# First transform stages of a long convolution: float32 operands in half-row pairs instead of rounded high and low parts

## The chip, the core and the metric

One core of one Trainium2 chip. The metric is the device time of one execution in microseconds, median of several runs; the kernel before was run three times. Lower is better. TensorE appears as PE, VectorE as DVE, ScalarE as ACT, GpSimd as POOL, SyncE as SP. The profile of the kernel before comes from one further execution.

## What is computed

The reference adds three parts over 2048 tokens of 512 channels. Only the first is touched by the change; the second fills most of TensorE's time.

```python
xn = _layernorm(A_q)
# A: gated long convolution
k_shift = sum over t of k_pad[:, t:t+S] * shift_k[:, 3 - t]      # 4 taps
kv = k_shift * v
y  = irfft(rfft(pad(kv)) * rfft(pad(ssm_k)))[:S] + kv * ssm_D    # 4096-point transforms by channel
a  = xn * y
# B: top-2 of 8 experts, D = 512, F = 1792
b  = sum over e of gate_e * (silu(xn @ w1[e]) @ w2[e])
out = A_q + a + b
```

## The kernel before, in words

**Experts.** `build` (L1073) runs a lead-in (loading, logits, routing) and then eight experts one after another (`expert`, L913). The tokens of each expert are gathered, transposed (`turn`, L840: tiles `xg`, `ptm` or `ptx`, `xh`, `xl`) and multiplied with weight slices (`weights`, L882: a slice `wraw` comes by SP's queue, ACT makes its rounded part `wh`, DVE the rest `wl`; for slices 1 to 5 of the first expert POOL makes `wl`). Every product is three float32r products (`mm6`, L902): high by high, high by low, low by high. ACT then makes `h` and `ht` from the product tile `ps`, of which there are two; so the product of a feature block f (48 matmuls for f=0 and f=1 together in the first expert) has to be read by ACT before that of f+2 can start.

**The convolution in the background.** The transforms are done as matrices: a first stage over 64 points (the filter by `conv_k`, L646; the gated tokens by `conv_v`, L682), a middle stage by 32 groups (`group_unit`, "g"), a last stage of 16 units (`last_unit`, "l"). After the last of these, `merge` adds what the experts left in `acc_d` to the output. From the twentieth feature block on, `fill` (L1138) hands out pieces of these units between the experts' matmuls, by the costs in `WORK`: the sum of all costs is spread evenly, and what is left when the last expert begins is issued at once. Six of the eight units of `conv_k` are issued earlier, in the lead-in and the routing, two in the background; all eight of `conv_v` are in the background. The scheduler then sets the order on each engine.

**The first stage of the filter.** A unit of `conv_k` transposes eight blocks of 128x128 (`ptk`), splits them into a rounded part `kh` (ACT) and a rest `kl` (DVE, or POOL in the three units before the routing, where ACT also makes an unrounded copy `kr`), and multiplies: four product tiles of 512 columns with three float32r matmuls each, 12 in all, with weights `ek` that hold zeros in one half of their rows.

**The first stage of the tokens.** A unit of `conv_v` makes the tile `kva` by eight DVE operations, splits it by halves of its partitions into two tiles `vp` (two ACT casts, two DVE subtractions L733), and multiplies (`stage1`, `edge1`): four product tiles with two float32r matmuls each, 8 in all. ACT evicts each product to `ev`, and SP stores it to `zk_d` or `zv_d`. `ptk`, the products and other small products share four PSUM tiles (pool `pc`); `kh`, `kl`, `kva`, `vp`, `ev` and the routing tables (`slots`) share seven SBUF tiles (tag `b4`).

**The lead-in.** DVE computes the routing in one long chain; TensorE makes its small products (`pw`, `ptab`); ACT computes one Exp (`gt`, L456); POOL gathers six blocks `xg`, makes two `wl` (L895) and normalizes 12 blocks of `x` (L317). Then DVE and ACT scale `xg` (L875, L873), TensorE transposes it and the first expert's matmuls (L910) begin.

Of the kernel before, what the change touches and what calls it, by code (L numbers as in the profile page):

```python
# [11 lines left out]
F32 = mybir.dt.float32  # L12
F32R = mybir.dt.float32r
# [5 lines left out]
P = 128  # L19
S = 2048  # L20
D = 512
DC = D // P
# [21 lines left out]
WORK = {"k": 1.7, "v": 12.6, "g": 5.0, "l": 2.8}  # L44
# [19 lines left out]
def fft_constants():  # L64
# [12 lines left out]
    fh, fl = _split(fwd.reshape(N1, P))  # L77
# [4 lines left out]
    zf, zi = np.zeros_like(fl), np.zeros_like(il)  # L82
    first = np.zeros((N1, 2, 2, 2, P), np.float32)
    for h in range(2):
        first[:, h, 0, h], first[:, h, 1, h] = fh, fl
    edge = np.concatenate([first.reshape(P, 4 * P), np.concatenate([fh, fh]), np.concatenate([fl, zf]),
                           np.concatenate([zf, fl]), il, ih, il, zi, ih, zi], axis=1)
# [57 lines left out]
class Builder:  # L145
# [47 lines left out]
    def load_x(self, ep, sp, cp):  # L193
# [139 lines left out]
    def routing(self, bp, sp, cp):  # L333
# [113 lines left out]
        for dc, c8 in ((1, 1), (2, 0), (2, 1)):  # L447
            for _ in self.conv_k(cp, dc, c8, True):
                pass
# [153 lines left out]
    def split_halves(self, pair, src):  # L603

        nc = self.nc
        halves = [slice(h * H, (h + 1) * H) for h in range(2)]
        for w, t in zip(halves, pair):
            nc.scalar.activation(t[w], src[w], AF.Copy)
        for w, o, t in zip(halves, halves[::-1], pair):
            nc.vector.tensor_sub(t[o], src[w], t[w])  # L610

    def edge1(self, out, h, pair):

        self.nc.tensor.matmul(out, self.ev[:, 0, :], pair[h], start=True, stop=False)
        self.nc.tensor.matmul(out, self.ev[:, 1 + h, :], pair[h], start=False, stop=True)
# [5 lines left out]
    def stage1(self, cp, pair, zd):  # L621
        nc = self.nc
        _, m, w = pair[0].shape
        for h in range(2):
            ev = cp.tile([P, m, w], F32, tag="b4", name="ev")
            for i in range(2):
                r = slice(i * m // 2, (i + 1) * m // 2)
                ps = self.pc.tile([P, m // 2, w], F32, tag="c", name="ps1")
                self.edge1(ps, h, [t[:, r, :] for t in pair])
                nc.scalar.activation(ev[:, r, :], ps, AF.Copy)  # L630
            nc.sync.dma_start(zd[h], ev)

    def load_k(self, cp, dc):

        nc, io = self.nc, self.io
        if dc == 0:
            self.dv = self.cp.tile([P, DC], F32, name="dv")
            nc.sync.dma_start(self.dv, io["A_ssm_D"].rearrange("(c p) -> p c", p=P))
        t = cp.tile([P, S], F32, tag="k8", name="ks", bufs=2)
        if dc == DC - 1:  # L640
            self.after(nc.gpsimd.memset(t[:1, :1], 0.0), self.gather, "the first expert's tokens come first")
        nc.sync.dma_start(t, io["A_ssm_k"][dc * P:(dc + 1) * P, :])
        nc.gpsimd.tensor_add(t[:, 0:1], t[:, 0:1], self.dv[:, dc:dc + 1])
        return t.rearrange("p (n i) -> p i n", i=NI)

    def conv_k(self, cp, dc, c8, routed):  # L646

        nc = self.nc
        if c8 == 0:
            self.ks = self.load_k(cp, dc)  # L650
        ks = self.ks
        parts = []
# [531 lines left out]
```

## Time and profile before

| | us |
|---|---|
| median of 3 runs | 884.62 (881.83 to 886.33) |
| the profiled execution | 887.87 |
| its span, first to last instruction | 885.9 |
| PE busy | 846.9 (96%) |
| DVE busy | 618.8 (70%) |
| ACT busy | 522.1 (59%) |
| POOL busy | 241.3 (27%) |

The span is from the first to the last instruction on the core; 2 us of the execution lie outside it. Busy times are summed over the span. A matmul's record is longer than the distance to the next one, since matmuls overlap at their ends: what a matmul costs TensorE is read from the distance of starts.

### The profile page before, as it was taken

The numbers are of one execution on the slowest core, as the hardware profiler recorded it, in microseconds if no ns is written. First come the engines' busy times: TensorE is split into PE (matmuls) and PEld (weight loads), VectorE is DVE, ScalarE is ACT, GpSimd is POOL, SyncE is SP. The second block draws the span as 40 slices with busy tenths as digits, with TensorE's granted clock in tenths as the row PEclk, the third lists the DMA queues.
The fourth block names the chain that finished last, engine by engine and source line by source line (L and its number), as shares of the span: only waits on it lengthen the run. The fifth ranks groups of instructions, "written<-read, shape, count | busy, mean of one in ns | idle before, by whom it ended". The sixth has DMA issues, their size and how long they took to land. (4 is left out here: it accounts for less than half of the span.)

```text
span 885.9 us, 13938 instructions
## 1 busy us (share of the span) xinstructions
PE 846.9 (96%) x5072; PEld 753.6 (85%) x5072; DVE 618.8 (70%) x867; ACT 522.1 (59%) x808; POOL 241.3 (27%) x209
## 2 busy tenths in 40 slices
PE   9849899999999999999999999999999999997996
PEld 7538899999999999899999888888888787885885
DVE  6977583499879988277775787577865866996421
ACT  4637342356644565477865877658865776775420
POOL 1383205055320723005020052123001401553422
PEclk9969999999999999999999999999999999998999
DMA  8569745988989675756676567558556738998972
GB/s 324 165 199 357 281 162 156 246 190 235 234 199 254 203 223 175 251 159 207 189 222 205 176 201 243 175 168 289 190 165 188 221 109 259 306 303 240 312 192 70
DMA packets 146641, 191.37 MB, mean 216 GB/s; under 512 B 12689, under 2 KB 106251, under 8 KB 145100
## 3 DMA queue, kind: packets, MB, share of 16 engines
q1 hardware_dynamic: 130204, 147.23, 54.3%
q0 software_dynamic: 16368, 43.24, 17.0%
q8 instruction: 41, 0.67, 0.3%
q14 instruction: 28, 0.23, 0.1%
HBM read 144.27 MB, written 50.63 MB: 220 GB/s over the span
## 5 line engine op out<-in xcount | busy, mean ns | idle before, releaser
L892 ACT ACTIVATE wh<-wraw 128x1024 fp32r<-128x1024 f32 (+1 forms) x116 | 119.4, 1030 | 140.9 <-PE ps L910 85.1
L895 DVE TENSOR_TENSOR wl<-wraw,wh 128x1024 fp32r<-128x1024 f32 (+1 forms) x111 | 131.7, 1187 | 97.8 <-ACT wh L892 88.8
L910 PE MATMUL ps<-xh,wh 128*128 128x512 f32 (+4 forms) x672 | 183.9, 327 | 6.3 <-ACT ht L937 5.9
L910 PE MATMUL ps<-xh,wl 128*128 128x512 f32 (+4 forms) x672 | 183.2, 326 | 0.0
L910 PE MATMUL ps<-xl,wh 128*128 128x512 f32 (+4 forms) x672 | 183.2, 326 | 0.0
L910 PE MATMUL ps<-h,wh 128*128 128x288 f32 (+3 forms) x896 | 155.2, 291 | 0.0
L910 PEld LDWEIGHTS ps<-h,wh 128*128 128x128 f32 x896 | 129.9, 188 | 1.7
L910 PEld LDWEIGHTS ps<-xh,wh 128*128 128x128 f32 x672 | 114.3, 190 | 17.7 <-ACT ht L937 7.5
L910 PEld LDWEIGHTS ps<-xh,wl 128*128 128x128 f32 x672 | 114.1, 190 | 9.6
L910 PEld LDWEIGHTS ps<-xl,wh 128*128 128x128 f32 x672 | 114.3, 190 | 9.2
L938 DVE TENSOR_TENSOR h<-ht,h 128x512 fp32r<-128x512 f32 (+4 forms) x112 | 81.7, 731 | 28.4 <-ACT ht L937 27.6
L936 ACT ACTIVATE h<-ps 128x512 fp32r<-128x512 f32 (+4 forms) x112 | 67.9, 606 | 53.5 <-PE ps L910 49.8
L910 PE MATMUL ps<-h,wl 128*128 128x288 f32 (+3 forms) x448 | 94.6, 290 | 0.0
L984 PE MATMUL py<-wh,h 128*128 128x512 f32 x224 | 87.6, 391 | 0.0
L983 PE MATMUL py<-wl,h 128*128 128x512 f32 x224 | 87.6, 391 | 0.0
L982 PE MATMUL py<-wh,h 128*128 128x512 f32 x224 | 87.1, 392 | 0.2 <-ACT ht L937 0.2
L964 POOL DMA_INDIRECT acc_d<-acc,ids x36 | 48.5, 1346 | 97.2 <-DVE acc L962 89.9
L835 POOL DMA_INDIRECT xg<-xn_d,gix x34 | 48.7, 1433 | 93.9 <-PE ptx L854 47.6
L910 PEld LDWEIGHTS ps<-h,wl 128*128 128x128 f32 x448 | 71.6, 189 | 0.5
L949 POOL DMA_INDIRECT acc<-acc_d,gix x36 | 44.2, 1227 | 96.6 <-PE ptx L854 59.6
L937 ACT ACTIVATE ht<-ps 128x512 f32<-128x512 f32 (+4 forms) x112 | 68.3, 609 | 0.0
L743 POOL DMA_DIRECT2D mid<-in_c_mid_dram x16 | 9.3, 580 | 163.5 <-PE pz L601 157.7
(256 smaller groups left out, 1409.5 us busy)
## 6 DMA issues: line engine op xcount, KB each, us to landing
wraw<-in_B_w_dram SPq DMA_DIRECT2D x84, 512.0 KB, 4.6
wraw<-in_B_w_dram SPq DMA_DIRECT2D x32, 448.0 KB, 3.8
zk_d<-ev SPq DMA_DIRECT2D x16, 512.0 KB, 7.0
zv_d<-ev SPq DMA_DIRECT2D x16, 512.0 KB, 8.7
mid<-in_c_mid_dram POOLq DMA_DIRECT2D x16, 512.0 KB, 4.6
z<-zk_d SPq DMA_DIRECT2D x32, 256.0 KB, 2.8
z<-zv_d SPq DMA_DIRECT2D x32, 256.0 KB, 3.5
zi_d<-zo SPq DMA_DIRECT2D x32, 256.0 KB, 3.3
```

The lines of the kernel that those rows point to most:

```text
L835: self.gather = nc.gpsimd.indirect_dma_start(out=t[:sb], out_offset=None, in_=self.xn_d[:, :] if r else self.io["A_q"].rearrange("o s d -> ...
L892: w = nc.scalar.activation(hi, raw, AF.Copy)
L895: t = (lo_eng or nc.vector).tensor_sub(lo, raw, hi)
L910: nc.tensor.matmul(ps[:, u, :n], w, x[:, u, :], start=first and w is wh and k == 0, stop=last and w is wl)
L936: nc.scalar.activation(h, ps[:, :nu, :n], AF.Silu)
L937: acts.append(nc.scalar.activation(t, ps[:, :nu, :n], AF.Silu))
L938: self.hid = nc.vector.tensor_sub(l, t, h)
L949: nc.gpsimd.indirect_dma_start(out=acc[:sb], out_offset=None, in_=sum_d[:, :], in_offset=bass.IndirectOffsetOnAxis(ap=self.gix[:sb, c0 + b ...
L964: st = nc.gpsimd.indirect_dma_start(out=sum_d[:, :], out_offset=bass.IndirectOffsetOnAxis(ap=self.ids[:sb, c0 + b:c0 + b + 1], axis=0), in ...
L982: nc.tensor.matmul(o, a, wh[:, f, :], start=ff == 0, stop=False)
L983: nc.tensor.matmul(o, a, wl[:, f, :], start=False, stop=False)
L984: nc.tensor.matmul(o, l, wh[:, f, :], start=False, stop=ff == FC - 1)
```

## The change

Both first stages now multiply float32 words. `kh`, `kl`, `kr`, `vp` and the split operations are gone: a unit of `conv_k` evicts its transposed block once, unrounded (`kt`), a unit of `conv_v` uses `kva` itself. A unit of `conv_k` now takes channels of two blocks of 128 together, the upper half of the partitions belonging to one and the lower to the other, and the two halves are multiplied by two matmuls that use 64 rows each (`ev[h, :]`, `src[h, r, :]`) and write two product tiles. Four such float32 matmuls of 512 columns make a unit. The filter is loaded two blocks at a time (one tile of 2 MB for two loads; the second pair waits for the gathers). Of the eight `conv_k` units, three come in the lead-in, three with the routing, two in the background, as before. The taps are loaded and turned one unit ahead. The weights `ek` are gone, `ev` is one tile of 64 KB and comes by SP's queue instead of POOL's. `ht` and `yt` share one tag of four tiles, and the costs for `fill` are new.

```diff
-WORK = {"k": 1.7, "v": 12.6, "g": 5.0, "l": 2.8}
+WORK = {"t": 1.2, "k": 0.6, "v": 10.2, "g": 5.0, "l": 2.8}
...
-        self.ek = cp.tile([P, 2, 2, P], F32R, name="ek", bufs=1)
-        self.ev = cp.tile([P, 3, P], F32R, name="ev", bufs=1)
-        edge = io["c_edge"]
-        nc.gpsimd.dma_start(self.ek, edge[:, :4 * P].rearrange("p (a c m) -> p a c m", a=2, c=2))
-        nc.gpsimd.dma_start(self.ev, edge[:, 4 * P:7 * P].rearrange("p (a m) -> p a m", a=3))
+        self.ev = cp.tile([P, P], F32, name="ev", bufs=1)
+        nc.sync.dma_start(self.ev, io["c_edge"][:, :P])
...
+    def pairs(self, cp, src, zd):
+        nc = self.nc
+        m, w = src.shape[1:]
+        halves = [slice(h * H, (h + 1) * H) for h in range(2)]
+        evs = [cp.tile([P, m, w], F32, tag="b4", name="ev") for _ in range(2)]
+        for i in range(2):
+            r = slice(i * m // 2, (i + 1) * m // 2)
+            ps = [self.pc.tile([P, m // 2, w], F32, tag="c", name="ps1") for _ in range(2)]
+            for t, h in zip(ps, halves):
+                nc.tensor.matmul(t, self.ev[h, :], src[h, r, :], start=True, stop=True)
+            for t, ev in zip(ps, evs):
+                nc.scalar.activation(ev[:, r, :], t, AF.Copy)
+        for ev, z in zip(evs, zd):
+            nc.sync.dma_start(z, ev)
...
+        t = cp.tile([P, 2, S], F32, tag="k8", name="ks", bufs=2)
+        for c in range(2):
+            dc = 2 * pair + c
+            if pair:
+                self.after(nc.gpsimd.memset(t[:1, c, :1], 0.0), self.gather, "the first expert's tokens come first")
+            nc.sync.dma_start(t[:, c, :], io["A_ssm_k"][dc * P:(dc + 1) * P, :])
+            nc.gpsimd.tensor_add(t[:, c, 0:1], t[:, c, 0:1], self.dv[:, dc:dc + 1])
...
+        kt = cp.tile([P, 8, P], F32, tag="b4", name="kt")
         for i in range(2):
             pt = self.pc.tile([P, 4, P], F32, tag="c", name="ptk")
             for u in range(4):
...
+            nc.scalar.activation(kt[:, 4 * i:4 * i + 4, :], pt, AF.Copy)
...
-        pair = [cp.tile([P, 4, DH], F32R, tag="b4", name="vp") for _ in range(2)]
-        halves = [slice(h * H, (h + 1) * H) for h in range(2)]
-        for w, t in zip(halves, pair):
-            nc.scalar.activation(t[w], a[w], AF.Copy)
-        for w, o, t in zip(halves, halves[::-1], pair):
-            nc.vector.tensor_sub(t[o], a[w], t[w])
-            yield 1.2
         yield
-        self.stage1(cp, pair, [self.zv_d[:, NI * h + 4 * c4:NI * h + 4 * c4 + 4, ds] for h in range(2)])
+        self.pairs(cp, a, [self.zv_d[:, NI * h + 4 * c4:NI * h + 4 * c4 + 4, ds] for h in range(2)])
...
-                t = hp.tile([P, nu, n], F32, tag="ht", name="ht", bufs=2)
+                t = hp.tile([P, nu, n], F32, tag="ht", name="ht", bufs=DC)
...
-            t = hp.tile([P, nu, n], F32, tag="yt", name="yt", bufs=DC)
+            t = hp.tile([P, nu, n], F32, tag="ht", name="yt", bufs=DC)
```

The order on the engines moves at three places. In the lead-in, POOL and ACT before (POOL first; `kl`, `kr`, `kh` belong to `conv_k`, `gt` is the Exp, `wh` a weight slice):

```order
L643 TENSOR_TENSOR ks<-ks,dv 128x1 x2
L669 TENSOR_TENSOR kl<-kr,kh 128x512 x5
L643 TENSOR_TENSOR ks<-ks,dv 128x1
L669 TENSOR_TENSOR kl<-kr,kh 128x512
L835 DMA xg<-in_A_q_dram,gix 96x512 x6
L662 ACTIVATE kh<-ptk 128x512 x2
L892 ACTIVATE wh<-wraw 128x1024 x2
L456 ACT_TABLE_LOAD
L456 ACTIVATE gt<-gt 128x16
L892 ACTIVATE wh<-wraw 128x1024
```

and now:

```order
L628 TENSOR_TENSOR ks<-ks,dv 128x1 x2
L809 DMA xg<-in_A_q_dram,gix 96x512 x6
L642 ACTIVATE kt<-ptk 128x512 x2
L866 ACTIVATE wh<-wraw 128x1024
L608 ACTIVATE ev<-ps_690 128x512
L608 ACTIVATE ev<-ps_691 128x512
L449 ACT_TABLE_LOAD
L449 ACTIVATE gt<-gt 128x16
```

POOL has no subtraction of `conv_k` ahead of its gathers any more, and the Exp stands behind one weight slice where it stood behind two.

On PE, from the transposes of the first expert's tokens (`ptm`) to its matmuls, before:

```order
L600 MATMUL ps_805<-kl,ek 128x512
L601 MATMUL ps_805<-kh,ek 128x512
L854 MATMUL ptm<-ident,xg 128x96 x6
L659 MATMUL ptk<-ident,ks 128x128 x8
L854 MATMUL ptm<-ident,xg 128x96 x6
L599 MATMUL ps_830<-kh,ek 128x512
L599 MATMUL ps_835<-kh,ek 128x512
L910 MATMUL ps<-xh,wh 128x288 x2
```

and now, inside the first expert (feature blocks f=0 and f=1 end where the first `ps_726` stands, f=2 begins behind `ps_762`):

```order
L641 MATMUL ptk<-ident,ks 128x128 x8
L884 MATMUL ps<-xl,wh 128x288
L884 MATMUL ps<-xh,wl 128x288 x2
L884 MATMUL ps<-xh,wh 128x288 x2
L884 MATMUL ps<-xl,wh 128x288 x2
L884 MATMUL ps<-xh,wl 128x288 x2
L606 MATMUL ps_726<-kt,ev 128x512
L606 MATMUL ps_727<-kt,ev 128x512
L606 MATMUL ps_732<-kt,ev 128x512
L606 MATMUL ps_733<-kt,ev 128x512
L641 MATMUL ptk<-ident,ks 128x128 x8
L606 MATMUL ps_755<-kt,ev 128x512
```

Two whole `conv_k` units have moved from before the first expert's matmuls to behind f=1, and between `ptm` and L884 nothing stands any more.

On POOL at the last expert (`xnb` is the product of a last-stage unit, `mt` and `out_dram<-mt` belong to `merge`), before:

```order
L813 TENSOR_TENSOR xnb<-xnb,yb 128x512 x10
L964 DMA acc_d<-acc,ids 2048x512 x4
L813 TENSOR_TENSOR xnb<-xnb,yb 128x512
L824 DMA mt<-acc_d 128x1024
L813 TENSOR_TENSOR xnb<-xnb,yb 128x512
L825 DMA out_dram<-mt 128x1024
L824 DMA mt<-acc_d 128x1024
L813 TENSOR_TENSOR xnb<-xnb,yb 128x512
```

and now:

```order
L787 TENSOR_TENSOR xnb<-xnb,yb 128x512 x16
L938 DMA acc_d<-acc,ids 2048x512 x4
L798 DMA mt<-acc_d 128x1024 x3
L799 DMA out_dram<-mt 128x1024 x3
L798 DMA mt<-acc_d 128x1024 x3
```

All sixteen products of the last stage now stand ahead of the seventh expert's stores and of `merge`; six of them stood among the transfers of `merge`.

## Rows read from the trace of the kernel before

**Rows 1.** Busy time by stretch: the stretch in us, its length, then for PE, PEld (weight load), DVE, ACT and POOL busy us and instructions, the granted clock as a share of 2.4 GHz, DMA share and GB/s.
```profile
180.00:360.00 180.00, 179.45 (x1385) 176.48 (x1385) 152.93 (x164) 99.32 (x154) 66.64 (x45) 1.00 0.82 214
390.00:800.00 410.00, 406.67 (x2131) 347.37 (x2130) 301.88 (x377) 293.65 (x446) 93.78 (x79) 1.00 0.67 213
800.00:820.00 20.00, 14.47 (x50) 10.36 (x50) 11.81 (x15) 9.88 (x16) 7.73 (x10) 0.85 0.80 233
```

**Rows 2.** The waits of PE, longest first: who waited for whom, us in total, times, the longest.
```profile
PE ptm L854 <- DVE xg L875: 10.2, 1, 10.2
PE ps L910 <- ACT ht L937: 5.9, 3, 4.5
```

**Rows 3.** The timeline of PE at full clock: start us, us, engine, line, operation, shapes and count. First a `conv_v` unit's float32r matmuls, then two float32 matmuls of the routing (each is one matmul in the program and two records in the trace), then a unit's transposes.
```profile
189.05 0.40 PE L614 MATMUL ps<-vp,ev 128*128 128x512 f32 x1
189.28 0.39 PE L615 MATMUL ps<-vp,ev 128*128 128x512 f32 x1
189.51 0.42 PE L910 MATMUL ps<-xh,wh 128*128 128x276 f32 x2
...
35.36 0.39 PE L380 MATMUL pw<-sel,rt 128*128 128x128 f32 x2
35.58 0.39 PE L381 MATMUL pw<-rt,cs 128*128 128x128 f32 x2
...
72.01 1.09 PE L659 MATMUL ptk<-ident,ks 128*128 128x128 f32 x8
```

**Rows 4.** Groups of PE instructions by line and shape: count, then busy us and mean ns of one, then idle time before.
```profile
L854 PE MATMUL ptx<-ident,xg 128*128 128x128 f32 x64 | 8.8, 272 | 0.0
L854 PE MATMUL ptx<-ident,xg 88*128 88x88 f32 x24 | 2.6, 239 | 0.0
```

**Rows 5.** The timeline of DVE in the lead-in; in brackets idle time before the row and who ended it.
```profile
28.46 0.29 DVE L362 TENSOR_TENSOR eq<-lgt,m 128x128 f32<-128x128 f32 x1
30.41 1.31 DVE L362 TENSOR_TENSOR eq<-L,m 128x128 f32<-128x128 f32 x1
31.64 1.25 DVE L454 TENSOR_TENSOR gt<-m,m 128x16 f32<-128x16 f32 x1
37.91 1.16 DVE L295 TENSOR_SCALAR rs<-mv 128x16 f32<-128x16 f32 x1
51.81 0.17 DVE L457 TENSOR_SCALAR gt<-gt 128x16 f32<-128x16 f32 x1 [4.25 <-ACT gt L456]
53.17 5.46 DVE L462 TENSOR_TENSOR gl<-gf,gh 128x32 f32<-128x32 f32 x1
62.50 0.16 DVE L442 COPY tb<-ptab 96x24 f32<-96x24 f32 x1
65.04 1.88 DVE L875 TENSOR_SCALAR xg<-xg,sc,sc 96x512 f32<-96x512 f32 x3
```

**Rows 6.** The timeline of POOL in the lead-in.
```profile
30.30 2.57 POOL L669 TENSOR_TENSOR kl<-kr,kh 128x512 fp32r<-128x512 f32 x2 [3.71 <-ACT kr L668]
37.75 1.28 POOL L669 TENSOR_TENSOR kl<-kr,kh 128x512 fp32r<-128x512 f32 x1
53.76 4.66 POOL L895 TENSOR_TENSOR wl<-wraw,wh 128x1024 fp32r<-128x1024 f32 x2
58.39 12.45 POOL L317 TENSOR_SCALAR x<-x,rstd,nmr 128x512 f32<-128x512 f32 x12
```

**Rows 7.** The timeline of ACT at the Exp and behind the first transposes.
```profile
45.61 1.06 ACT L892 ACTIVATE wh<-wraw 128x1024 fp32r<-128x1024 f32 x1 [2.81 <-DMA wraw<-in_B_w_dram]
49.20 1.06 ACT L892 ACTIVATE wh<-wraw 128x1024 fp32r<-128x1024 f32 x1 [2.52 <-DMA wraw<-in_B_w_dram]
74.25 2.94 ACT L314 ACTIVATE x<-x,nmr,rstd 128x512 f32<-128x512 f32 x4
```

**Rows 8.** The timeline of PE from the transposes of the tokens on: the k matmuls between them, the first matmuls of the first expert, and f=2, which begins at 82.58.
```profile
65.76 2.18 PE L854 MATMUL ptm<-ident,xg 96*128 96x96 f32 x12 [10.16 <-DVE xg L875]
67.65 1.20 PE L599 MATMUL ps<-kh,ek 128*128 128x512 f32 x2
...
71.51 0.66 PE L854 MATMUL ptm<-ident,xg 96*128 96x96 f32 x6
...
73.96 0.42 PE L910 MATMUL ps<-xh,wh 128*128 128x288 f32 x2
...
82.58 0.42 PE L910 MATMUL ps<-xh,wh 128*128 128x288 f32 x2
```

**Rows 9.** DMA issues: operation, count, KB each, median us from issue to landing.
```profile
ks<-in_A_ssm_k_dram SPq DMA_DIRECT2D x4, 1024.0 KB, 14.0
```

**Rows 10.** The timeline of POOL, ACT and PE at the last expert.
```profile
810.54 0.97 POOL L825 DMA_DIRECT2D out_dram<-mt  x1 [6.57 <-DMA xnb<-xn_d]
811.74 1.64 POOL L813 TENSOR_TENSOR xnb<-xnb,yb 128x512 f32<-128x512 f32 x1
813.41 1.21 ACT L810 ACTIVATE yb<-psb 64x512 f32<-64x512 f32 x2 [5.18 <-POOL xnb L813]
815.77 0.80 PE L910 MATMUL ps<-xh,wh 128*128 128x512 f32 x1 [4.47 <-ACT ht L937]
816.80 0.63 PE L910 MATMUL ps<-xh,wl 128*128 128x512 f32 x1
820.64 0.43 PE L910 MATMUL ps<-xh,wl 128*128 128x512 f32 x1
```

More of the change, by code (lines that the diff above doesn't have):

```diff
@@ L81, in fft_constants @@
     ih, il = _split(inv.reshape(P, N1))
[L82 to L87, printed above, removed]
+    zi = np.zeros_like(il)
+    f = fwd.reshape(N1, P).astype(np.float32)
+    edge = np.concatenate([np.concatenate([f, f]), il, ih, il, zi, ih, zi], axis=1)
     n2 = np.arange(N2)
@@ L446, in routing @@
         self.prep(0)
-        for dc, c8 in ((1, 1), (2, 0), (2, 1)):
-            for _ in self.conv_k(cp, dc, c8, True):
+        for pair, q8 in ((0, 3), (1, 0), (1, 1)):
+            for _ in self.conv_k(cp, pair, q8):
                 pass
@@ L617, in tokens @@
     def tokens(self, ap):
         return ap.rearrange("(n h j) d -> h n j d", h=2, j=NI)
[L621 to L631, printed above, removed]
@@ L633, in load_k @@
-    def load_k(self, cp, dc):
+    def load_k(self, cp, pair):
         nc, io = self.nc, self.io
-        if dc == 0:
+        if pair == 0:
             self.dv = self.cp.tile([P, DC], F32, name="dv")
             nc.sync.dma_start(self.dv, io["A_ssm_D"].rearrange("(c p) -> p c", p=P))
[L639 to L644, printed above, removed]
@@ L658, in conv_k @@
             for u in range(4):
-                nc.tensor.transpose(pt[:, u, :], ks[:, 8 * c8 + 4 * i + u, :], self.ident)
-            if routed:
-                hi, lo = (t[:, r, :] for t in big)
-                nc.scalar.activation(hi, pt, AF.Copy)
-                self.after(nc.vector.tensor_sub(lo, pt, hi), self.indexed, "the routing comes first")
-            else:
-                hi, lo, raw = (self.xp.tile([P, 4, P], d, tag="xg", name=n, bufs=10)
-                               for d, n in ((F32R, "kh"), (F32R, "kl"), (F32, "kr")))
-                nc.scalar.activation(hi, pt, AF.Copy)
-                nc.scalar.activation(raw, pt, AF.Copy)
-                nc.gpsimd.tensor_sub(lo, raw, hi)
@@ new lines, in conv_k, with load_taps @@
+            nc.scalar.activation(kt[:, 4 * i:4 * i + 4, :], pt, AF.Copy)
+        yield 0.3
+        yield
+        self.pairs(cp, kt, [self.zk_d[:, 8 * q8:8 * q8 + 8, dc * P:(dc + 1) * P] for dc in (2 * pair, 2 * pair + 1)])
+        yield 0.3
+    def load_taps(self, cp, dh):
+        ds = slice(dh * DH, (dh + 1) * DH)
+        self.sr = cp.tile([P, DH, 4], F32, tag="b4", name="shr")
+        self.nc.sync.dma_start(self.sr,
+                               self.io["A_shift_k"][ds].rearrange("(o d) t -> o d t", o=1).to_broadcast([P, DH, 4]))
@@ L707, in conv_v @@
         yield
-        if sr is not None:
-            self.sb = cp.tile([P, 4, DH], F32, tag="sb", name="sb", bufs=1)
-            nc.vector.tensor_copy(self.sb, sr.rearrange("p d t -> p t d"))
+        if dh == 1 and c4 == 0:
+            self.turn_taps(cp)
             yield 1.2
@@ L1109, in build @@
             slots = self.slots(cp)
-            units = [("k", lambda c8=c8: self.conv_k(cp, 3, c8, True)) for c8 in range(2)]
+            units = [("t", lambda: self.first_taps(cp))]
+            units += [("k", lambda q8=q8: self.conv_k(cp, 1, q8)) for q8 in (2, 3)]
             units += [("v", lambda dh=dh, c4=c4: self.conv_v(cp, dh, c4)) for dh in range(2) for c4 in range(4)]
```

52 lines of the change are left out of this document (19 added, 33 removed).

## The prediction

> **What bounds the kernel now.** I read the busy time by stretch first. Between 180 and 360 us PE is busy 179.45 of 180 us, between 390 and 800 us 406.67 of 410, at full clock [rows 1]: there the number of matmuls and their distance set the time, 1385 in 179.45 us or 0.13 us for one of the usual shape. DVE has 152.93 of the first 180 us: what it loses there (two subtractions per token unit) is hidden behind PE, and ACT, with 99.32, likewise; I cost those splits at nothing. The waits of PE come second: the longest is 10.2 us for the first expert's scaled tokens, the next 5.9 us for ACT, of which 4.5 are one wait [rows 2]. So the time has three handles: the matmul work after the first expert starts, the moment at which it starts, and that one wait near the end.
>
> **Matmul work.** Starts of the token unit's float32r matmuls lie 0.23 us apart [rows 3]. A token unit (8) costs 1.84 us, a filter unit (12) 2.76. Float32: one matmul of the program is two records, and two of them with 128 columns lie 0.22 us apart, so a record takes 0.11 [rows 3]. [...] A record of 512 columns then takes 0.44 us, a float32 matmul 0.88, and a unit of four 3.52 us if everything runs one behind the other. [...]
>
> The two matmuls of a pair use different halves of the array's rows and write different product tiles, and no wait stands between them. No row of this trace shows whether such matmuls overlap. If order on PE is kept, the second record of one can run beside the first record of the next: eight records take five slots of 0.44, 2.2 us a unit. Between 2.2 and 3.52 I take 2.2, since a matmul waits only for the one ahead to stream, not for its end (0.39 long, 0.23 apart [rows 3]), and in another half of the array nothing streams that it must wait for.
>
> [...]
>
> With 2.2 the eight token units cost 8 x 0.36 = **2.9 us more**, the two late filter units 2 x 0.56 = **1.1 us less**. Serially it is 8 x 1.68 = 13.4 more and 2 x 0.76 = 1.5 more. Against the change stands the passage from full-height to half-height matmuls and back: no row has one. Between nothing and the overlap of two neighbours lost twice (0.39 - 0.23 = 0.16 us [rows 3]) for 12 groups, that is 0 to 3.8 us; passages between matmuls and transposes show no gap at all, so I take **1.0**.
>
> [...]
>
> **The start of the first expert.** Look at DVE: the same comparison takes 0.29 us at 28.46 and 1.31 at 30.41, and two operations on 16 columns take 1.25 and 1.16 [rows 5]. Each falls into a subtraction `kl` of POOL [rows 6]; all of these are gone from POOL. I count 1.0 + 1.0 + 0.9 = 2.9 us off the chain. Next, DVE waits 4.25 us for the Exp [rows 5], which stood behind two weight casts, at 45.61 and 49.20 [rows 7], and now stands behind one: about 3.6 us earlier. Then one operation of 32 columns takes 5.46 us [rows 5] while POOL makes two `wl` [rows 6]. POOL does these behind the gathers, so they end 2.9 us earlier too, at about 55.5, but DVE by then has the rows behind the Exp done; before, it had them ahead of it, and came to the scale factors only at 62.50. Last, the three scalings of `xg`, 65.04 to 66.92 in one piece before, are now spread among some 17 small routing rows and four of 0.4 us (the scheduler's order on DVE), so that the last ends at about 62: 5 us earlier, not more. Behind it, before, 7.0 us passed until 73.96, of which 3.9 were filter matmuls between the transposes (67.65 to 71.51) [rows 8]. Those are gone from there; about 12 small DVE rows come in (1.6). So the first expert starts at 62 + 7.0 - 3.9 + 1.6 = **66.7 instead of 73.96**. Ends: only the 2.9, or 11 if DVE meets no wait for POOL.
>
> That gain isn't kept. Two filter units now stand between f=1 and f=2, and f=2 is the first point where both kernels have done the same. Before: 82.58 [rows 8]. Now 66.7, plus 48 matmuls of 0.13 (6.3), plus twice the transposes (8 in 1.09 us, 0.94 without the last one's tail [rows 3]) and a unit (2.2), 6.3 together: 79.3. To this come waits. ACT has the `x` blocks (2.94 us, rows 7), a table load and four evictions ahead of the second unit's, in one queue with the `h` of f=0 that f=2 waits for. And the filter's second pair is loaded late: SP issues it behind the read of the overflow count, about 58, and such a load took 14.0 us [rows 9], so it lands at 72 to 73 where PE wants it at 73. POOL's correction of it waits for 12.45 us of normalizing [rows 6], to about 68: hidden. I take 2.2 us (bounds 0 and 6): f=2 at 81.5, **1.1 us less** than before. With serial matmuls it is 2 x 1.32 more, of which the queue of ACT takes up a good half of the waits: about 84, 1.8 more. The stalls behind f=2, on routing tables, I leave as they are.
>
> **Near the end.** The 4.5 us wait is at 815.77: PE waits for `ht`, ACT for the tile that POOL's `xnb` frees (5.18 us), and POOL, in order, sits 6.57 us in front of a transfer of `merge` for a DMA [rows 10]. In the new order all sixteen `xnb` stand ahead of `merge`, because the last units fit before the last expert. [...] Eleven matmuls at 0.2 are 2.2. Together **6.7 less** (bounds 0 and 7). What is late next is `merge`, which starts behind all `xnb`; it has the last expert's 70 us to finish.
>
> The taps a unit ahead, `ev` by SP and four tiles for `ht` touch waits for ACT of which 1.4 us is left beside the long one [rows 2]; I cost them at nothing.
>
> **Sum**, overlapped: 2.9 - 1.1 + 1.0 - 1.1 - 6.7 = -5.0 us. The profiled execution took 887.87, 3.25 above the median of 884.62; I apply the difference to the median: **879.6**. From no change, 0.5% (4.4 us) is about what a measurement of this kernel tells.
>
> **Rivals.**
> *Serial records* (slower side). The second half-row matmul waits for the first: 13.4 + 1.5 + 1.8 + 1.0 - 6.7 = +11.0, **895.6**. For it: the records of one float32 matmul run one behind the other, and none beside another [rows 3]. Against: halves and tiles are disjoint. It decides by the cost of one float32 matmul in a saturated stretch: the sum is zero where it is some 0.68 us (the 40 late ones then take 27 us, 7 more than the 20.2 of before), 0.55 is my forecast, 0.88 the rival.
> *The end wait stays.* The last units again meet `merge`, or pile up one expert earlier, where they wait for the same two tiles: 879.6 + 6.7 = **886.3**. For it: the order is a schedule, and a unit that is late by some us meets the transfers again. Against: `xnb` stand in front of every transfer of `merge`.
> *The start is kept.* DVE and ACT run ahead enough that f=2 comes 7 us earlier as the first expert does, 6 less than summed: **873.6**; or records cost less than 0.44, which leads the same way (at 0.23 the ten late units alone would give 14 us less). For it: five us of DVE's chain are waits only. Against: ACT's queue, in which the `h` of f=0 stands last.
>
> **Numbers.** Forecast 0.47, own range 874 to 885; serial 0.25; end wait 0.15; start kept or cheap records 0.13. Faster by over 0.5% (below 880.2): somewhat over half of the forecast and all of the last, 0.40. Slower (above 889.0): most of the serial case and a little of the others, 0.25. Within: 0.35. The range goes from 870 (half of the best case left out) to 897 (a third of the serial case left out).
>
> **What would show it.** Starts of `ps<-kva,ev` records: the next pair's in the same half 0.9 us on and the partner's beside the second record means overlap; 0.44 between all means serial. `kl` gone and no DVE operation over 1 us at 30 to 38; the first L884 at 66 to 67; f=2 at 80 to 83; no wait over 2 us for `ht` near 810. I'd be wrong in the main step if half-row records follow one another, in the second if the first expert starts after 71, in the third if PE stands for ACT at the last expert as before.

## The result: 0.7% slower, and the first expert late

The kernel with the change takes 893.0 us (median of 14 runs, 889.78 to 895.03), the kernel before beside it 886.22: ratio 1.0071, 95% interval 1.0048 to 1.0093. In a later session it took 893.86, ratio 1.0087 (1.0058 to 1.0117). The forecast was 879.6, with a range of 870 to 897: the time lies inside the range, but it moved the other way. The profiled execution has a span of 891.1 us against 885.9, 5.2 more.

### The profile after

First the matmul work and the end. Busy time by stretch, columns as in [rows 1]; the profile gives the granted clock as a share of full speed, and no run shows a frequency:

```profile
180.00:360.00 180.00, 176.58 (x1296) 160.66 (x1295) 134.12 (x148) 85.55 (x145) 63.05 (x40) 0.99 0.79 218
800.00:820.00 20.00, 18.25 (x81) 14.82 (x80) 12.68 (x15) 9.27 (x14) 9.44 (x10) 1.00 0.83 258
```

Between 800 and 820 PE is busy 18.25 us at full clock, where it had 14.47 at 0.85: the wait for `ht` at the last expert is gone. The 1.75 us that PE still stands there are one wait for DVE's `acc` at 807.28, which is new. The waits of PE, to be laid beside [rows 2]:

```profile
PE ptm L828 <- DVE xg L849: 24.5, 3, 22.1
PE ps L884 <- ACT ht L911: 2.9, 2, 1.9
PE pk L592 <- ACT hi L584: 2.3, 1, 2.3
PE psb L781 <- ACT hi L584: 2.2, 2, 2.0
```

The 4.5 us for `ht` are gone. The wait for the first expert's tokens has grown from 10.2 to 24.5. Two of about 2 us, where the first middle-stage unit and the first last-stage unit begin, had 1.7 and 1.1 before.

The timeline of PE: a token unit in one piece, and one that the scheduler cut up with matmuls of the expert (compare [rows 3]):

```profile
218.47 0.41 PE L884 MATMUL ps<-xh,wl 128*128 128x276 f32 x2
218.81 1.99 PE L606 MATMUL ps<-kva,ev 64*128 64x512 f32 x8
220.73 0.52 PE L884 MATMUL ps<-xh,wh 128*128 128x276 f32 x2
221.09 0.42 PE L884 MATMUL ps<-xl,wh 128*128 128x276 f32 x2
...
183.89 1.12 PE L606 MATMUL ps<-kva,ev 64*128 64x512 f32 x2
184.94 0.40 PE L884 MATMUL ps<-h,wh 128*128 128x288 f32 x1
185.27 1.12 PE L606 MATMUL ps<-kva,ev 64*128 64x512 f32 x2
...
186.65 1.13 PE L606 MATMUL ps<-kva,ev 64*128 64x512 f32 x4
187.71 0.40 PE L884 MATMUL ps<-h,wh 128*128 128x288 f32 x1
```

The row at 218.81 merges eight records, which take 1.92 us to the next start at 220.73. Taken one by one in the trace, they start in pairs: 218.81 and 218.82, 219.34 and 219.35, 219.77 and 219.78, 220.20 and 220.21. So the two matmuls of a pair run beside each other from their first records on. In the cut unit one float32 matmul alone (two records) takes 1.05 us (183.89 to 184.94), and the two of a pair side by side take 1.06 (four records, 186.65 to 187.71).

From the first transposes of the first expert's tokens to f=2 (compare [rows 8]):

```profile
65.64 0.90 PE L828 MATMUL ptm<-ident,xg 96*128 96x96 f32 x4 [22.12 <-DVE xg L849]
...
75.00 0.85 PE L884 MATMUL ps<-xh,wh 128*128 128x288 f32 x2 [0.57 <-DVE xl L835]
75.65 0.68 PE L884 MATMUL ps<-xl,wh 128*128 128x288 f32 x2
76.13 0.68 PE L884 MATMUL ps<-xh,wl 128*128 128x288 f32 x2
...
78.36 0.43 PE L884 MATMUL ps<-xl,wh 128*128 128x288 f32 x2
...
87.63 1.99 PE L606 MATMUL ps<-kt,ev 64*128 64x512 f32 x8 [0.69 <-ACT kt L642]
91.51 0.63 PE L884 MATMUL ps<-xh,wh 128*128 128x288 f32 x2 [1.89 <-ACT ht L911]
```

The first expert starts at 75.00 (before 73.96), f=2 at 91.51 (before 82.58). After the stall PE runs at half clock until 78 (granted clock 0.50 over 70 to 75, 0.69 over 75 to 80): 0.48 us for two matmuls (75.65 to 76.13) instead of 0.26. Before, f=0 began at full clock (granted 1.00 over 70 to 75): PE had transposes and filter matmuls from 65.76 on, which no longer stand there.

DVE in the lead-in (compare [rows 5]):

```profile
29.53 0.29 DVE L355 TENSOR_TENSOR eq<-L,m 128x128 f32<-128x128 f32 x1
29.74 0.17 DVE L447 TENSOR_TENSOR gt<-m,m 128x16 f32<-128x16 f32 x1
45.65 0.33 DVE L450 TENSOR_SCALAR gt<-gt 128x16 f32<-128x16 f32 x1 [3.44 <-ACT gt L449]
47.13 0.18 DVE L455 TENSOR_TENSOR gl<-gf,gh 128x32 f32<-128x32 f32 x1
48.32 0.22 DVE L438 TENSOR_TENSOR sc<-tb 96x6 f32<-96x6 f32 x2
51.13 14.02 DVE L511 TENSOR_SCALAR ef<-ef 1x32 f32<-1x32 f32 x1
65.06 0.53 DVE L849 TENSOR_SCALAR xg<-xg,sc,sc 96x512 f32<-96x512 f32 x1
69.21 0.54 DVE L849 TENSOR_SCALAR xg<-xg,sc,sc 96x512 f32<-96x512 f32 x1
```

and POOL beside it (compare [rows 6]; the last row is the twelfth of the twelve norms by itself):

```profile
48.75 2.72 POOL L809 DMA_INDIRECT xg<-in_A_q_dram,gix  x1 [0.30 <-issue]
51.53 0.73 POOL L683 MEMSET k<- 1x768 f32 x1
52.23 4.63 POOL L869 TENSOR_TENSOR wl<-wraw,wh 128x1024 fp32r<-128x1024 f32 x2
56.86 9.72 POOL L310 TENSOR_SCALAR x<-x,rstd,nmr 128x512 f32<-128x512 f32 x12
65.10 1.47 POOL L310 TENSOR_SCALAR x<-x,rstd,nmr 128x512 f32<-128x512 f32 x1
```

The short rows that had taken 1.2 to 1.3 us are back at 0.2 to 0.3, `gl` takes 0.18 instead of 5.46, and the scale factors are ready at 48.5 instead of 63.6: DVE's chain is 15 us ahead. Then one minimum over 32 numbers takes 14.02 us (before, 0.16). It begins while POOL issues the last gather and ends as the twelfth norm begins; eleven norms pass at 0.76 us each. The three scalings stand behind it.

Summed over TensorE, from f=2 to the last matmul, distance of starts less idle time:

| us | before | after |
|---|---|---|
| two late filter units | 5.53 | 3.84 |
| eight token units | 14.80 | 18.67 |
| waits | 14.95 | 9.41 |
| all other matmuls | 759.98 | 759.89 |

That is 3.4 us less. All that was lost lies ahead of f=2, 8.9 us.

### The profile page after: what moved, and what is told of

Read it like the earlier page. It is cut to its first block, busy times and chain, and to the rows that moved or that the text cites. A ratio compares the mean times of both kernels' runs of the same rounds, so it can differ in the third digit from the quotient of the medians.

```text
span 891.1 us, 13814 instructions
## 1 busy us (share of the span) xinstructions
PE 840.8 (94%) x5040; PEld 734.6 (82%) x5040; DVE 599.9 (67%) x841; ACT 501.0 (56%) x786; POOL 234.1 (26%) x202
## 5 line engine op out<-in xcount | busy, mean ns | idle before, releaser
L869 DVE TENSOR_TENSOR wl<-wraw,wh 128x1024 fp32r<-128x1024 f32 (+1 forms) x111 | 135.0, 1216 | 110.1 <-ACT wh L866 99.9
L884 PE MATMUL ps<-xh,wh 128*128 128x512 f32 (+4 forms) x672 | 183.8, 328 | 5.6 <-ACT ht L911 2.9
L884 PE MATMUL ps<-xl,wh 128*128 128x512 f32 (+4 forms) x672 | 182.8, 326 | 0.0
L884 PE MATMUL ps<-xh,wl 128*128 128x512 f32 (+4 forms) x672 | 182.0, 325 | 0.0
L884 PE MATMUL ps<-h,wh 128*128 128x288 f32 (+3 forms) x896 | 154.3, 291 | 0.0
L884 PEld LDWEIGHTS ps<-h,wh 128*128 128x128 f32 x896 | 129.0, 189 | 5.6 <-issue 4.5
L884 PEld LDWEIGHTS ps<-xh,wh 128*128 128x128 f32 x672 | 113.7, 190 | 22.1 <-ACT ht L911 5.1
L884 PEld LDWEIGHTS ps<-xl,wh 128*128 128x128 f32 x672 | 114.2, 190 | 8.7
L884 PEld LDWEIGHTS ps<-xh,wl 128*128 128x128 f32 x672 | 113.8, 190 | 9.0
L912 DVE TENSOR_TENSOR h<-ht,h 128x512 fp32r<-128x512 f32 (+4 forms) x112 | 79.7, 717 | 44.3 <-ACT ht L911 44.1
L884 PE MATMUL ps<-h,wl 128*128 128x288 f32 (+3 forms) x448 | 95.5, 291 | 0.0
L938 POOL DMA_INDIRECT acc_d<-acc,ids x36 | 54.0, 1499 | 120.7 <-DVE acc L936 114.0
L884 PEld LDWEIGHTS ps<-h,wl 128*128 128x128 f32 x448 | 71.7, 189 | 1.9 <-issue 1.5
L923 POOL DMA_INDIRECT acc<-acc_d,gix x36 | 46.8, 1300 | 99.1 <-PE ptx L828 64.3
L809 POOL DMA_INDIRECT xg<-xn_d,gix x34 | 41.4, 1218 | 82.2 <-PE ptx L828 40.6
L738 DVE TENSOR_TENSOR ka<-pu,ka 128x512 f32<-128x512 f32 x32 | 22.1, 691 | 50.5 <-ACT ka L733 43.2
```

What stands on the lines that cost most here:

```text
L809: self.gather = nc.gpsimd.indirect_dma_start(out=t[:sb], out_offset=None, in_=self.xn_d[:, :] if r else self.io["A_q"].rearrange("o s d -> ...
L869: t = (lo_eng or nc.vector).tensor_sub(lo, raw, hi)
L884: nc.tensor.matmul(ps[:, u, :n], w, x[:, u, :], start=first and w is wh and k == 0, stop=last and w is wl)
L912: self.hid = nc.vector.tensor_sub(l, t, h)
L923: nc.gpsimd.indirect_dma_start(out=acc[:sb], out_offset=None, in_=sum_d[:, :], in_offset=bass.IndirectOffsetOnAxis(ap=self.gix[:sb, c0 + b ...
L938: st = nc.gpsimd.indirect_dma_start(out=sum_d[:, :], out_offset=bass.IndirectOffsetOnAxis(ap=self.ids[:sb, c0 + b:c0 + b + 1], axis=0), in ...
```

## The experiments

Theory A: POOL's unbroken queue (memsets, two `wl`, twelve normalizations of `x`, called norms here) holds the DVE instruction that is pending, and the scalings behind it. Theory B: the gathers, of which the last lands at 57.6, set the start. Further theories, on why the hold is so long, came with the runs. All edits are against the kernel with the change, unless said otherwise.

### POOL's work taken out of the way

The norms ordered behind the split of the first tokens:

```diff
-                    self.pool_norms.append(t)
+                    self.pool_norms.append(t); self.after(t, self.parted, "the first expert comes first")
```

> The twelve normalizations of POOL wait until the first expert's tokens are split; nothing else is changed against the kernel with the change. Theory A (POOL's unbroken queue of two wl and twelve norms holds the VectorE instruction that is pending, and all behind it): L511 ends when the wl end, at about 57, and lasts some 6 us instead of 14.02; the scalings of xg follow 8 us earlier, the first expert starts at 66 to 68 instead of 75.0, f=2 at 83 to 86 instead of 91.5, and the kernel takes 884 to 887 us, 6 to 9 less than with the change. Theory B (the scalings wait for the gathers, whose last lands at 57.6, and for the small routing rows between them; POOL only looks guilty): VectorE still stands until 62 or later, the start stays at 73 or later, the time at 891 or more.

882.4 us, ratio to the kernel before 0.9948 (0.9917 to 0.9979), 10.6 under the median with the change. The hint moves the order only: the norms stood behind a correction of `ks`, and that waited for its transfer. DVE's timeline:

```profile
50.44 5.78 DVE L511 TENSOR_SCALAR ef<-ef 1x32 f32<-1x32 f32 x1
```

POOL's:

```profile
61.39 0.24 POOL L628 TENSOR_TENSOR ks<-ks,dv 128x1 f32<-128x1 f32 x1 [5.21 <-DMA ks<-in_A_ssm_k_dram]
61.61 9.15 POOL L310 TENSOR_SCALAR x<-x,rstd,nmr 128x512 f32<-128x512 f32 x12
```

PE's:

```profile
66.89 0.85 PE L884 MATMUL ps<-xh,wh 128*128 128x288 f32 x2 [0.57 <-DVE xl L835]
```

Theory A's numbers for the hold, which ends with the two `wl`, and for the start, 8.1 us earlier; f=2 comes at 84.54, and the time is 1.6 us below its range.

The other half of the queue, the two `wl`, given to DVE:

```diff
-                                  nc.gpsimd if r == 0 and 0 < s < 6 else None,
+                                  nc.gpsimd if r == 0 and 2 < s < 6 else None,
```

> The low parts of slices 1 and 2 of the first expert's weights are made by VectorE instead of POOL; the norms stay where they are, behind them. Theory A: VectorE has about 2.4 us more to do and isn't held by the two wl; it may still be held by the norms, 9.1 us in a row from about 55: a single VectorE row of 5 to 9 us stands somewhere between 54 and 64, the first expert starts at 68 to 73, time 886 to 891. If the norms alternate with VectorE as they did in the kernel before, no row over 1.5 us is seen, the start is at 63 to 66 and the time 881 to 885. Theory B: start at 73 or later, 891 or more.

879.22 us, ratio 0.992 (0.9893 to 0.9948). DVE's timeline, with the norms beside it from 52.63 on:

```profile
53.94 0.92 DVE L849 TENSOR_SCALAR xg<-xg,sc,sc 96x512 f32<-96x512 f32 x1
```

PE's:

```profile
64.15 0.85 PE L884 MATMUL ps<-xh,wh 128*128 128x288 f32 x2 [1.11 <-DVE xl L835]
```

No DVE instruction over 1.5 us is left: DVE and the norms alternate, 0.92 us for a scaling that takes 0.53 alone. This is the second of theory A's cases; the start is 10.9 us earlier, f=2 at 80.08, and the time 1.8 us below its range.

Both edits together:

> Both: the norms wait until the first expert's tokens are split, and the low parts of slices 1 and 2 are made by VectorE, so that POOL has nothing between the gathers and that split but two memsets. Theory A: no VectorE row over 1.3 us between 50 and 64; the last gather, at 57.6, sets the start now, and the first expert starts at 63 to 65, within a microsecond of the kernel with the low parts alone moved (64.15), because there the norms already alternated with VectorE; time 877 to 881. If the alternating norms cost what the rows of 0.9 us show: start at 61 to 62.5, time 874 to 877. What speaks against a gain: the norms come later, so the stores of x and the first token unit's loads do too, and POOL's second correction of ks may come behind them after PE wants it.

880.46 us, ratio 0.9938 (0.9915 to 0.9961). The start comes at 62.85, between the two expectations, and is lost again: the second correction of `ks` now stands behind the norms and PE waits 1.24 us for it, f=2 at 81.13. The last gather sets the start here (ACT's scaling of it begins at 57.28), so theory B holds only once POOL is out of the way.

### What is held, and how long

L511 put behind the split, so that another instruction stands in its place:

```diff
-        V.tensor_scalar_min(ef, ef, float(E - 1))
+        self.after(V.tensor_scalar_min(ef, ef, float(E - 1)), self.parted, "the first expert comes first")
```

> The one instruction that took 14.02 us, L511 on 1x32, is put behind the split of the first expert's tokens; nothing else moves. Theory A: whichever VectorE instruction stands there next is held as long: the first scaling of xg (or the row behind it) takes 13 to 14 us, the start stays at 74 to 76, time within 1.5 us of the kernel with the change. Theory C (this instruction, on one partition, is what gets stuck): no row of 5 us or more is left on VectorE between 50 and 66, the scalings are done by 59 to 60, the first expert starts at 64 to 67, time 882 to 886.

888.66 us, ratio 1.0016 (0.9982 to 1.0049), start at 68.92. Neither theory's number: an instruction is held, but by the two `wl` alone, and later rows alternate with the norms. DVE's timeline:

```profile
52.07 5.07 DVE L479 TENSOR_TENSOR wk<-oh,col 128x256 f32<-128x256 f32 x1
```

POOL's memset of the token tile `k`, ahead of the two `wl`:

```profile
51.42 0.73 POOL L683 MEMSET k<- 1x768 f32 x1
```

So A was incomplete. Three runs ask what makes the long hold: the form (`V.tensor_tensor(ef, ef, self.e7, op=ALU.min)`, with `e7` a tile of sevens), the partitions (`ec`, `ef`, `en` as tiles of P rows instead of one), and chance.

> L511 makes the same 1x32 minimum as a TENSOR_TENSOR against a tile of sevens instead of a TENSOR_SCALAR with a constant; POOL's queue and the order on VectorE stay. Seen so far: a TENSOR_TENSOR that was pending in this place was held 5.07 us, by the two wl alone, the TENSOR_SCALAR L511 14.02 us, by the norms too. Theory D (the form of the held instruction decides whether the norms pass it over): L511 is held 5 to 6 us, ends near 57, the first expert starts at 67 to 70, time 882 to 889. Theory E (the form has no part in it; what is pending at that point is held until POOL's queue has a gap): about 14 us again, the start at 74 to 76, time 891 to 895.

> The chain that ends in L511 runs on 128 partitions instead of one (the same sizes in a partition, so the same length), order and forms as with the change. The instructions that got out behind the two wl (before: 128x32, with the 1x32 chain behind the norms: 128x256) were on 128 partitions. Theory F (an instruction on one partition is passed over by the norms): L511 is held 5 to 6 us and ends near 57, the first expert starts at 67 to 70, time 884 to 889. If the number of partitions has no part in it: 14 us again, start 74 to 76, 891 to 895. Against F speaks the kernel with the token units alone, where a 1x8 instruction got out after 5.42 us.

> The kernel with the change once more, beside the next three on the same chip. If the long hold belongs to the order of the two queues, L511 takes 14.0 us again, released ahead of the last norm, the first expert starts at 74 to 76, time 891 to 895. If it was a chance of one execution: L511 under 7 us and a start at 67 to 70.

Form: 892.97 us, L511 held 14.07 us. Partitions: 893.66, held 14.03. The same kernel again: 893.86, held 14.03. Form, partitions and chance are out. What differs from the kernel before in the order of the two `wl` and the norms on POOL is one short memset of the first token tile, which the change's earlier units moved ahead of the two `wl` (before, it stood behind the norms):

```diff
-            nc.gpsimd.memset(k[0:1, :3, :], 0.0)
+            self.after(nc.gpsimd.memset(k[0:1, :3, :], 0.0), self.parted, "the first expert comes first")
```

> POOL's memset of the first token tile k, 0.73 us, which the change moved ahead of the two wl, goes behind the norms again, as in the kernel before; the order on VectorE and TensorE stays. Theory G (VectorE's pending instruction is held only to the end of the wl where it meets nothing but short work ahead of them, and past the norms where the memset stands there): L511 is held 5 to 6 us and ends near 56, the first expert starts at 66 to 70, time 882 to 889. If the memset has no part in it: 13 to 14 us again, start 73 to 75, 890 to 895.

889.48 us, ratio 1.003 (1.0004 to 1.0057). DVE's order and PE's are the same to the row; on POOL only the memset moved, on SP two loads changed places. DVE's timeline:

```profile
50.41 5.38 DVE L511 TENSOR_SCALAR ef<-ef 1x32 f32<-1x32 f32 x1
62.25 0.94 DVE L849 TENSOR_SCALAR xg<-xg,sc,sc 96x512 f32<-96x512 f32 x1
```

POOL's:

```profile
50.75 0.12 POOL L626 MEMSET ks<- 1x1 f32 x2
50.84 4.64 POOL L869 TENSOR_TENSOR wl<-wraw,wh 128x1024 fp32r<-128x1024 f32 x2
55.48 10.68 POOL L310 TENSOR_SCALAR x<-x,rstd,nmr 128x512 f32<-128x512 f32 x12
```

PE's:

```profile
70.00 0.85 PE L884 MATMUL ps<-xh,wh 128*128 128x288 f32 x2 [0.57 <-DVE xl L835]
```

Theory G holds for the hold and the start: 5.38 us instead of 14.02, 5.0 us earlier; the time is 0.5 us above its range. Moving a memset of 0.73 us brings f=2 to 87.82, 3.7 us earlier, and the median 3.5 us down; the two intervals of the ratio overlap slightly, so the time alone would not show it.

The memset in the queue is not enough for the long hold. In each long hold DVE's instruction began 0.40 us before this memset. With L511 put behind the split the held instruction began after it (52.07 against 51.42) and was held by the two `wl` only. The full-height kernel below has the queue of the change too, later by 5 us. Its POOL and DVE:

```profile
56.45 0.73 POOL L683 MEMSET k<- 1x768 f32 x1
56.59 5.74 DVE L849 TENSOR_SCALAR xg<-xg,sc,sc 96x512 f32<-96x512 f32 x1 [1.26 <-DMA xg<-in_A_q_dram,gix]
```

There too DVE's instruction began behind the memset's start, and the norms alternated with DVE after the `wl`. No run varies this order by itself, so it is a pattern of the runs and not a shown cause.

Eight norms on POOL instead of twelve (`if j > 1` for `if j == 3`):

> ScalarE makes eight of the sixteen norms instead of four, POOL the other eight. In three executions with twelve the hold ended ahead of the last norm, 14.03 us after it began. If POOL gives way when only its last instruction without a wait is left: the hold ends ahead of the eighth norm, 3.0 us earlier, and lasts 11.0 us. If it lasts a fixed time: 14 us, past the end of the norms. The first expert starts 3 us earlier in the first case; the time is a single one and may hide it, since ScalarE has 2.9 us more in front of the first h.

891.79 us in one run. The hold lasts 11.80 us and goes with the length of the queue, but it ends behind the eighth norm, ahead of the correction of `ks`, not ahead of the last norm as expected. By what rule POOL gives way stays open.

### The price of the matmuls

Against the kernel before, the token units alone in float32 pairs (`conv_v` and its cost, 10.2 in `WORK`, as with the change; `conv_k` as before):

```diff
-        self.stage1(cp, pair, [self.zv_d[:, NI * h + 4 * c4:NI * h + 4 * c4 + 4, ds] for h in range(2)])
+        self.pairs(cp, a, [self.zv_d[:, NI * h + 4 * c4:NI * h + 4 * c4 + 4, ds] for h in range(2)])
```

> The kernel before with the token units alone in float32 pairs (and their planned cost); the filter stays rounded and low, so the lead-in is that of before. If the two terms that came out behind f=2 belong to the token units and to the order near the end that their smaller plan gives: first expert at 74, f=2 at 82.6 as before, a token unit at 1.9 to 2.0 us, no wait over 2 us for ht near 810, and 880 to 883 us, 3 to 6 under the kernel before. If the end wait went because of the filter's or the new buffers' part of the change: the 4 to 5 us wait near 810 is still there, and the time is 886 to 888.

888.58 us, ratio 1.0028 (0.9995 to 1.0061), a miss: f=2 at 81.61 and no wait over 2 us for `ht` near 810, as expected, yet no gain. By distance of starts the token units cost 17.44 us against 14.80. Part of the rest is late next, where the middle and the last stage begin; the waits of PE there, 4.4 us in place of 2.8:

```profile
PE psb L816 <- ACT hi L591: 2.6, 1, 2.6
PE pk L599 <- DVE lo L594: 1.8, 1, 1.8
```

Behind the first of them PE falls to half clock (granted 0.83 over 720 to 730 us, records of 0.63 us instead of 0.39 at 726.64), and behind the second, near 350, likewise (0.63 at 349.43). A third stretch, two matmuls in 0.48 us from 97.25 to 100.13, is there in the kernel before too (97.64 to 100.05). So the half clock behind f=2 adds up to 10.2 us again, three times 3.4, as before (3.4 and 6.8): what the end gave back is lost at two other places. With the change there is one stretch like these two, at 344 us (granted 0.83 over 340 to 350).

The overlap taken away, each matmul over all 128 rows:

```diff
-            for t, h in zip(ps, halves):
-                nc.tensor.matmul(t, self.ev[h, :], src[h, r, :], start=True, stop=True)
+            for t in ps:
+                nc.tensor.matmul(t, self.ev, src[:, r, :], start=True, stop=True)
```

> Each float32 matmul of a pair takes all 128 rows and no second one runs beside it (it multiplies both halves into one sum: what the stage makes is left wrong, its count and size of matmuls are the same). If the side-by-side run of two half-row records is what makes a unit 1.92 us: a unit of eight records takes 3.5 us, the eight token units and four late filter units give 12 x 1.6 = 19 us, less what waits in the lead-in take up, and the time is 906 to 912. If a record of 512 float32 columns is cheap by itself: 1.9 to 2.0 us a unit and 892 to 895.

900.04 us, ratio 1.0164 (1.0144 to 1.0184). PE's timeline:

```profile
157.41 3.60 PE L606 MATMUL ps<-kt,ev 128*128 128x512 f32 x8
160.44 0.70 PE L884 MATMUL ps<-h,wl 128*128 128x288 f32 x1
160.98 0.69 PE L884 MATMUL ps<-h,wh 128*128 128x288 f32 x4
```

A unit takes 3.44 us (157.41 to 160.98 less one L884 of 0.13) against 1.92, or 2.10 with the passages ahead of it and behind it (218.47 to 221.09 less four L884): the side-by-side run is what makes it cheap. The time is 6 us below the expectation: at full height a cut unit costs no more than a whole one, while half-row matmuls lose their partner there (one and an L884 take 0.99 us at full height, 187.94 to 188.93, and 1.38 over half the rows, 183.89 to 185.27); and the half clock behind f=2 (two matmuls in 0.26 us at 95.11, where the change has 0.48 at 91.93) and the wait at 344 us are gone, though a half clock near 740 us is new (records of 0.63 at 738.94 and 739.36).

### A faster version

The filter's second pair loaded with the first (`if pair > 1:` for `if pair:` in `load_k`), beside both edits to POOL:

> As the kernel with both moves, and the filter's second pair of rows is loaded at the start with the first, not behind the gathers, so that all eight filter units run ahead of the first expert. Theory B (2 MB of filter loads beside the gathers make the last one land late): the last gather lands 3 to 5 us earlier, the first expert starts at 59 to 62; f=2 has no filter unit ahead of it any more (6.3 us and the waits for ACT less) and starts 12.5 us behind the first, at 72 to 75, and the time is 869 to 875. If the loads at the start come ahead of the token blocks and the logits are late for it: the start moves back by 3 to 5 us, and the time is 877 or more.

877.32 us, ratio 0.991 (0.988 to 0.994), but the start at 70.30, which neither case gave: no correction of `ks` held the norms back now, so they ran from 49.63 on, 14.78 us in alternation with DVE. With a true wait instead of a hint (the norms read `held`, a copy of `nmr` that ACT makes behind the split), first without and then with the early load:

> The norms read a copy of nmr that ScalarE makes behind the split of the first expert's tokens, so they really wait for it (before, only their order was moved, behind a correction of ks), and the low parts of slices 1 and 2 are on VectorE. The first expert starts at 62 to 64 as with the norms moved and the low parts on VectorE (62.85), f=2 at 79 to 82, time 877 to 881: nothing but the last gather (57.3) bounds the start, so an emptier POOL gives no more.

> The same, and the filter's second pair of rows loaded with the first, so that its four units run ahead of the first expert. With the pair loaded early and the norms alternating with VectorE the start was 70.30; now the norms are out of the way. If VectorE's alternation cost that start (15 us of norms among its rows): first expert at 63 to 66, f=2 at 76 to 79, time 868 to 873. If ScalarE and TensorE, busy with the four filter units until 58, cost it: the start stays at 68 or later and the time at 875 to 879.

Without the early load 882.18 us, 1.2 above its range, ratio 0.9955 (0.9932 to 0.9977), start 63.42, f=2 81.76 behind a wait of 1.66 us for the correction of `ks`. With it **871.32 us, ratio 0.9845 (0.9803 to 0.9888)**, faster than both kernels. POOL's timeline:

```profile
63.80 10.28 POOL L310 TENSOR_SCALAR x<-x,rstd,held 128x512 f32<-128x512 f32 x12 [11.59 <-ACT held L300]
```

PE's:

```profile
63.47 0.85 PE L884 MATMUL ps<-xh,wh 128*128 128x288 f32 x2 [0.57 <-DVE xl L835]
...
72.41 0.42 PE L884 MATMUL ps<-xh,wh 128*128 128x288 f32 x2
```

The start is the same as without the early load (63.42), and the last gather lands at 57.67 where it landed at 57.82 with the load beside it: the load did not delay the gathers, and that part of theory B is refuted. The gain is that no filter unit and no wait for ACT stand between f=1 and f=2, which begins at 72.41, 9.4 us earlier.

## Why the prediction failed

**Matmul work: right, with sizes off both ways.** The overlap is there, and it is fuller than the prediction had it: it put the second record of one matmul beside the first record of the next, five slots of 0.44 us, and the trace has both records of a pair side by side, four slots in 1.92 us where 2.2 was the forecast. A late filter unit costs the same (1.7 us less for both, forecast 1.1 less). The eight token units cost 3.9 us more, forecast 2.9: whole, they would have cost 0.6 more, but three of them were cut and lost the overlap of a pair (1.05 us for one matmul alone), 3.3 us. The passage between heights shows as 0.08 us ahead of a unit and 0.10 behind it (218.47 to 221.09). Taken for each of the 14 pieces, that is an estimate of 2.5 us, where 1.0 of 0 to 3.8 was taken. What this cost consists of the trace does not show. The rival of serial records is refuted as a course of this kernel, though its 895.6 is near the 893.0; its price, 3.52 for a unit, was right (3.44 at full height). The 0.44 us of a record was the author's estimate, four times the 0.11 of [rows 3]; at full height the eight records of a unit take 0.43 each, and the 33 ns for 40 columns of [rows 4] would give 0.42.

**The end: right.** Of the 6.7 us, 4.5 are the wait at 815.77 [rows 10], and 2.2 are eleven records behind it at 0.2 more each: from 816.37 to 820.64 in the kernel before they start 0.43 us apart (granted clock 0.50 over 815 to 819), at full clock 0.23. The wait for `ht` and the half clock behind it are gone, and they are gone with the token units alone too, so neither the filter's part of the change nor the four tiles for `ht` was needed for it. Around it three things moved that the sum has at nothing: 3.5 us of waits for the routing tables behind f=2 went, where the two later stages begin PE waits 4.5 us in place of 2.8, with 3.4 us of half clock behind the wait at 344 us (granted 0.59 over 344 to 346, 0.55 over 346 to 348), and 1.75 us of waiting for `acc` are new at the last expert.

**The start of the first expert: the step that failed.** The chain to the scale factors went as written, and faster: 15 us ahead. The step says that the last scaling ends at about 62 because POOL's `wl` end at 55.5 and "DVE by then has the rows behind the Exp done". It had: `gl` takes 0.18 us. But DVE then met the same queue with L511, one row ahead of the three scalings, and the last scaling ended at 69.75. The step took for granted that DVE loses no time to the two `wl` and the twelve norms any more. Both of its bounds, 2.9 us and 11 us, were gains; a later start was in neither. The runs split the error at the start: with the norms out of the way it is 66.89; with the norms alternating 70.00, 3.1 more; with the memset ahead of the `wl` 75.00, another 5.0. That 66.89 meets the forecast of 66.7 is partly luck: the last scaling ends at 60.8 there instead of 62, and from it to the start it takes 6.1 us instead of 4.7.

**From the start to f=2** a smaller term was put at nothing. The prediction has the 48 matmuls of f=0 and f=1 at 0.13 us, full clock; but the filter matmuls that kept PE busy ahead of them had been moved away, and the first 14 ran at half clock: 1.5 of the 1.7 us by which 16.5 us exceed the 14.8. No run puts them back by themselves; with the token units alone, where they stand as before, the first expert's first matmuls, from 72.93 on, take 0.26 us for two. It does not go with the hold: where the memset is moved and the hold is 5.38 us, two matmuls take 0.48 us from 70.65 to 75.93, and with the norms out of the way f=2 is 17.65 us behind the start. The late second pair of the filter, on the other hand, cost nothing: its first load landed at 62.1 and not at 72 to 73. At f=2 that makes 91.51 - 81.5 = 10.0 us, of which 8.3 are the start; and the span came out 5.2 longer where 5.0 shorter was forecast, so the other terms nearly cancel.

What could have been seen: [rows 5] has `gl` held for 5.46 us, and the order on POOL with the change shows `MEMSET k`, two `wl` and twelve norms without a wait between them. I read the hold as the length of two instructions that DVE would have passed, not as a queue that may pass DVE by. No row of the kernel before shows a hold by norms as well: there DVE got in between them, and the twelve took 12.45 us [rows 6] where they take 9.15 alone. A loss for one instruction the runs show too (a scaling takes 0.92 us instead of 0.53 beside a norm); that DVE may be kept out over three memsets, two `wl` and eleven norms in a row, 14.02 us, no row of the kernel before shows.

Against the kernel before beside them, the kernel with the norms moved is 3.8 us faster and the one with the low parts on VectorE 7.0. The forecast of 5.0 lies between: without the long hold the change gains about what was forecast, but as a sum of terms that were off both ways.

## What to carry to other kernels

When a change takes work off the chain of one engine, look at what the engine meets when it arrives earlier: here DVE came 15 us sooner, just ahead of POOL's longest unbroken run. And look at what a piece of work did where it stood: the filter matmuls that were moved away had kept TensorE at work ahead of the first expert, which began at full clock with them (granted 1.00 over 70 to 75) and at half clock without (0.50). Plan a queue of POOL instructions without a wait between them as one obstacle with the length of the whole queue (here up to 14.07 us) until a run shows that the engines alternate, as with the `wl` on DVE (no DVE instruction over 1.5 us). Put such work behind a real wait, an operand that is written late: with the early load the first expert started at 63.47 behind such a wait and at 70.30 behind an ordering hint. Last, let nothing stand between two half-row matmuls that are meant to run side by side: one alone took 1.05 us, the two together 1.06.

## What was not expected of the hardware

- A DVE instruction of 0.16 us was held 14.02, 14.03, 14.07 and 14.03 us in four executions with the same POOL queue, whatever its form or its partitions, and 5.38 us when a memset of 0.73 us left that queue. With the memset in the queue, but DVE's instruction beginning after the memset's start, the hold was 5.07 and 5.74 us. Why eleven norms pass it in one case and none in the others is not settled.
- A float32 matmul of 512 columns over 64 rows takes 1.05 us alone and 1.06 us with a partner in the other rows, which starts 0.01 us behind it; four in a run take 1.92, where four over all 128 rows take 3.44.
